# Seven block products for eight in two projections of a fused attention, gating and rotation kernel

## The chip, the core and the metric

The kernel runs on one NeuronCore of a Trainium2 chip. The metric is the device time of one execution in microseconds (us), lower is better. Engines: TensorE (PE) multiplies and transposes, VectorE (DVE) and ScalarE (ACT) work element by element, GpSimd (POOL) too, SyncE (SP) issues the DMAs. Each engine works through its own list in order; semaphores tie the lists together.

## The reference

B = 8 batches of S = 576 tokens, model width 512. Cut to what is computed:

```python
# attention, twice: packed queries p over k, v; then q over the result
x = softmax(q @ softmax(p @ k.T / 8) @ v ...)            # per head, 8 heads x 64
# gating: h = relu(x @ w_in); u, v = halves of h
v_n = (v - mean(v)) / sqrt(var(v) + 1e-6)
x = (u * (w_spatial @ v_n + b_spatial)) @ w_out          # [B, 576, 512]
# rotation and mixing
theta = x @ w_theta
y = w_tok_r @ (x * cos(theta)) + w_tok_i @ (x * sin(theta))
u = x + y
out = u + relu(u @ w_ch)
```

## The kernel before

Phase 1 (about 0 to 337 us) computes the attention and the gating for each batch and stores the gated activations G, transposed, in DRAM (`Gd`, one tensor for each pair of batches). Beside it the weights, which come as 64-bit words, are turned into f32 (`cvt_tasks`, L616 to L625) and split.

f32 accuracy comes from splitting: every value is the sum of a rounded part (hi, L182, ACT) and a rest (lo, L185, DVE or POOL), and a product is three matmuls: hi hi, hi lo, lo hi.

Phase 2 (337 us to the end) runs over 36 tiles of 128 tokens: four pairs of batches, each in nine blocks of which block 4 holds the last 64 tokens of both batches. For a tile:

- `x_half`, twice: G's hi and lo (`GH`, loaded from `Gd` by `load_g`, L859, and split) times `WX`, which holds w_out and w_out @ w_theta / 2 pi side by side, 12 matmuls of 512 columns in one PSUM bank. ACT copies x out (L886); DVE takes the angle's fraction (L892, L893) and its absolute value (L895), ACT two sines (L897, L899), DVE multiplies by x (L911), ACT and DVE or POOL split the result into `z`. All of it 256 columns wide.
- `mix` (L919): all blocks of a batch times a 128-column slice of the resident weights `WR` (real and imaginary part, hi and lo; two loads of 2304 KB, L802), 27 matmuls, 18 for the 64-row block; DVE adds the bank to x (L939, L943).
- `turn` (L951): four transposes, split into `uT`. `chan` (L956): 12 matmuls with w_ch (`WC`); DVE forms u + relu (L977), SP stores the tile (L972).

The order of the work is set by `Plan`, a list scheduler that runs while the program is built: each task has an engine, a cost, a due key, operands and buffers, and of the tasks that can start soonest the one with the lowest key is written out next. `SHIFT` (L31) adds a number to the key of a named group of tasks; it is empty here. `step` gives phase 2 its keys: X (both halves of a tile), M (mix and turn) and C (chan).

Of the kernel before, what the change touches and what calls it, by code (L numbers as in the profile page):

```python
# [30 lines left out]
SHIFT = {}  # L31
# [144 lines left out]
def moe_kernel(ctx: ExitStack, tc, qT, kT, v, pT, w_in, wsT, bs, w_out,  # L176
# [10 lines left out]
    def mm(out, lhsT, rhs, start, stop):  # L187
        PE.matmul(out, lhsT, rhs, start=start, stop=stop)  # L188
# [30 lines left out]
    WRd = [dram.tile([9 * 128, S], F32, name=f"WRd{i}") for i in range(2)]  # L219
# [4 lines left out]
    WX = [const.tile([128, 4, 4, 2, 128], F32R, name=f"WX{i}") for i in range(2)]  # L224
# [16 lines left out]
    woT = wsp.tile([128, 4, DM], F32, name="woT")  # L241
    wth = wsp.tile([128, 4, DM], F32, name="wth")
# [5 lines left out]
    junk = apm.tile([128, 512], F32, name="junk")  # L248
# [36 lines left out]
    R_woT, R_wth = fixed(4), fixed(4)  # L285
    R_WX, R_wrd, R_gd = Res(), fixed(2), fixed(NPAIR)
# [200 lines left out]
    def v_part(b, key):  # L487
# [4 lines left out]
        for j in range(5):  # L492
# [23 lines left out]
            def centre(j=j):  # L516
# [158 lines left out]
    def wo_part(k, key):  # L675
        raw, g, ps = P.res("raw"), P.res("cvg"), P.res("bank")
# [29 lines left out]
    def wr_part(k, key):  # L706
# [15 lines left out]
        def st():  # L722
            for i in range(2):
                SP.dma_start(out=WRd[i][k * 128:(k + 1) * 128, :], in_=raw.t[:, i * S:(i + 1) * S])
        P.add("SP", 1.1, st, key + 5, r=[raw], w=R_wrd, size=590e3)

    def wcomb(kt, key):
        ps, wc = P.res("bank"), P.res("cvg")

        def f():  # L730
            for m in range(4):
                mm(ps.t, woT[:, m, kt * 128:(kt + 1) * 128], wth[:, m, :], m == 0, m == 3)
        rx = Res()
        wv = lambda: wc.t[:, 0:DM].rearrange("p (d n) -> p d n", d=4)
        P.add("PE", 3.45, f, key, r=[R_woT[kt], *R_wth], new=[ps])
        P.add("ACT", 0.62, lambda: A.activation(out=wc.t[:, 0:DM], in_=ps.t, func=AF.Copy, scale=1.0 / (2 * math.pi)),
              key + 1, r=[ps], new=[wc])
        P.add("ACT", 0.62, lambda: hi(WX[0][:, kt, :, 1, :], wv()), key + 2, r=[wc], w=[rx, R_WX])
        P.add(TT, 0, lambda e: lo(WX[1][:, kt, :, 1, :], wv(), WX[0][:, kt, :, 1, :], ENG[e]), key + 3, r=[wc, rx], w=[R_WX],
              port=True)  # L740
# [32 lines left out]
    cv += [(wr_part, k) for k in range(9)]  # L773
    for n, (f, k) in enumerate(cv):
        P.group = n
        f(k, at(0, 20 + 12.5 * n))
    for kt in range(4):
        P.group = kt
        wcomb(kt, at(7, 18 + kt))

# [15 lines left out]
    def load_wr(i):  # L796
        wp = gpool(f"wr{i}")
        if not i:
            WR64.append(wp.tile([128, 9, 128], F32R, name="WR64"))
        WR.append(wp.tile([128, 9, 512], F32R, name=f"WR{i}"))  # L800
        x = WRd[i].rearrange("(k p) t -> p k t", p=128)
        SP.dma_start(out=WR[i].bitcast(F32), in_=x[:, :, 0:512])  # L802
        SP.dma_start(out=WR64[0][:, :, i * 64:i * 64 + 64].bitcast(F32), in_=x[:, :, 512:576])

    def close1():
        lbd.close()
        gp = gpool("gp")
# [3 lines left out]
    for k in range(4):
        raw = P.res("raw")

        def ld(k=k, raw=raw):
            SP.dma_start(out=raw.t, in_=Gd[0][k * 128:(k + 1) * 128, :])
        P.add("SP", 0.6, ld, at(7, 1), r=[R_gd[0]], new=[raw], size=590e3, after=[c1])
        for o in range(2):
            c, rh = slice(o * S, (o + 1) * S), Res()
            P.add("ACT", 0.69, lambda k=k, c=c, raw=raw: hi(GH[0][:, k, c], raw.t[:, c]), at(7, 20 + 2 * k + o),
                  r=[raw], w=[rh, *R_G[o:o + 2]])  # L820
            P.add("DVE", 0.76, lambda k=k, c=c, raw=raw: lo(GH[1][:, k, c], raw.t[:, c], GH[0][:, k, c]),
                  at(7, 20 + 2 * k + o), r=[raw, rh], w=R_G[o:o + 2], port=True)
# [28 lines left out]
    def load_g(p, i, key):

        c = (slice(0, 640), slice(640, 1152))[i]
        rg = R_G[0:2] if i == 0 else R_G[2:3]
        w = c.stop - c.start
        rr = fixed(4)

        def ld():
            SP.dma_start(out=GH[1][:, :, c].bitcast(F32), in_=Gd[p][:, c].rearrange("(k p) t -> p k t", p=128))  # L859
        P.add("SP", 0.6, ld, key, r=[R_gd[p]], w=[*rg, *rr], size=512 * w * 4)  # L860
        for k in range(4):
            rh = Res()
            P.add("ACT", 0.1 + w * 1.04e-3, lambda k=k: hi(GH[0][:, k, c], GH[1][:, k, c].bitcast(F32)),
                  key + 6, r=[rr[k]], w=[rh, *rg])
            P.add({"POOL": w * 2.9e-3, "DVE": 0.16 + w * 1.04e-3}, 0,
                  lambda e, k=k: lo(GH[1][:, k, c], GH[1][:, k, c].bitcast(F32), GH[0][:, k, c], ENG[e]),
                  key + 6, r=[rr[k], rh], w=rg, port=True)
# [241 lines left out]
```

## Time and profile before

| | |
|---|---|
| median of 3 runs | 882.81 us (882.39 to 882.88) |
| span of the profiled execution | 880.3 us |
| PE busy in it | 857.8 us |
| DVE, ACT, POOL busy | 555.4, 396.6, 128.8 us |
| moved by DMA | 85.98 MB, mean 98 GB/s |

The table is of one profiled execution, and 882.81 - 880.3 = 2.5 us of the median lie outside its span. Matmuls overlap, so the mean duration of one is longer than the pitch at which they follow one another; the pitch is read from the chain of waits. An engine's idle time counts only where PE waits for it.

### The profile page before, as it was taken

The numbers are of one execution on the slowest core, as the hardware profiler recorded it, in microseconds if no ns is written. First come the engines' busy times: TensorE is split into PE (matmuls) and PEld (weight loads), VectorE is DVE, ScalarE is ACT, GpSimd is POOL, SyncE is SP. The second block draws the span as 40 slices with busy tenths as digits, with TensorE's granted clock in tenths as the row PEclk, the third lists the DMA queues.
The fourth block names the chain that finished last, engine by engine and source line by source line (L and its number), as shares of the span: only waits on it lengthen the run. The fifth ranks groups of instructions, "written<-read, shape, count | busy, mean of one in ns | idle before, by whom it ended". The sixth has DMA issues, their size and how long they took to land.

```text
span 880.3 us, 14428 instructions
## 1 busy us (share of the span) xinstructions
PE 857.8 (97%) x5552; PEld 707.4 (80%) x5552; DVE 555.4 (63%) x1278; ACT 396.6 (45%) x947; POOL 128.8 (15%) x115
## 2 busy tenths in 40 slices
PE   5879999999999999999999999999999999999998
PEld 2458888889888878888888888888888888888886
DVE  5889989989847625878733752752762662652522
ACT  4777876777746633654411530520440530440300
POOL 1641103123345110122100100000100000000000
PEclk9699999999999999999999999999999999999999
DMA  9974565866400835110101200201100200000101
GB/s 332 344 258 160 179 212 202 262 207 222 150 28 28 283 104 167 60 48 1 48 1 36 84 1 25 72 1 36 66 20 16 82 0 25 36 1 0 48 1 60
DMA packets 48441, 85.98 MB, mean 98 GB/s; under 512 B 8050, under 2 KB 18546, under 8 KB 48372
## 3 DMA queue, kind: packets, MB, share of 16 engines
q1 hardware_dynamic: 48372, 85.05, 28.9%
q8 instruction: 44, 0.72, 0.3%
q14 instruction: 25, 0.20, 0.1%
HBM read 60.85 MB, written 24.18 MB: 97 GB/s over the span
## 4 chain that ended last, share of the span: by engine, by line
PE 94%; DVE 3%; ACT 1%; DMA 1%; issue 0%; SPq 0%; DVEq 0%; ACTq 0%
PE bank L188 91%; PE bank L951 2%; PE bank L372 1%; DMA woT<-w_in 1%; DVE WIN L625 0%; DMA kt<-kT 0%; ACT a L364 0%; DVE wth L621 0%; DVE one L358 0%; PE bank L691 0%; DVE t L457 0%; DVE M L185 0%; PE bank L399 0%; DVE sm L465 0%; DVE ln L509 0%
## 5 line engine op out<-in xcount | busy, mean ns | idle before, releaser
L188 PE MATMUL bank<-z,WR 128*128 128x512 f32 x1008 | 236.2, 392 | 0.0
L188 PEld LDWEIGHTS bank<-z,WR 128*128 128x128 f32 x1008 | 187.6, 188 | 38.3
L188 PE MATMUL bank<-WX,GH 128*128 128x512 f32 x864 | 200.4, 390 | 0.0
L188 PEld LDWEIGHTS bank<-WX,GH 128*128 128x128 f32 x864 | 161.5, 188 | 33.2
L182 ACT ACTIVATE uT<-bank 128x512 fp32r<-128x512 f32 x36 | 21.5, 598 | 216.9 <-PE bank L951 204.2
L188 PE MATMUL bank<-WS,VN 128*128 128x288 f32 x768 | 115.8, 298 | 0.0
L188 PEld LDWEIGHTS bank<-WS,VN 128*128 128x128 f32 x768 | 105.8, 188 | 8.2 <-issue 4.3
L188 PE MATMUL bank<-WC,uT 128*128 128x512 f32 x432 | 103.0, 391 | 0.0
L188 PEld LDWEIGHTS bank<-WC,uT 128*128 128x128 f32 x432 | 80.6, 188 | 16.6
L939 DVE TENSOR_TENSOR xs<-bank,xs 128x512 f32<-128x512 f32 x32 | 22.1, 691 | 112.1 <-PE bank L188 112.1
L185 POOL TENSOR_TENSOR z<-ab,z 128x256 fp32r<-128x256 f32 x24 | 17.7, 738 | 377.1 <-ACT z L182 377.1
L188 PE MATMUL bank<-M,at 128*128 128x512 f32 x240 | 59.6, 402 | 0.0
L897 ACT ACTIVATE ab<-ab,halfpi 128x256 f32<-128x256 f32 x72 | 36.6, 508 | 47.2 <-DVE ab L895 47.0
L188 PE MATMUL bank<-at,M 128*128 128x288 f32 x384 | 55.9, 301 | 0.0
L977 DVE SCALAR_TENSOR_TENSOR xs<-bank,xs 128x512 f32<-128x512 f32 (+1 forms) x37 | 25.0, 677 | 47.4 <-PE bank L188 47.4
L188 PEld LDWEIGHTS bank<-M,at 128*128 128x128 f32 x240 | 45.0, 192 | 12.1 <-issue 2.0
L188 PEld LDWEIGHTS bank<-at,M 128*128 128x128 f32 x384 | 51.9, 188 | 1.6 <-issue 1.0
L886 ACT ACTIVATE xs<-bank 128x256 f32<-128x256 f32 x72 | 26.9, 380 | 57.2 <-PE bank L188 43.1
L892 DVE TENSOR_SCALAR fr<-bank 128x256 f32<-128x256 f32 x72 | 30.3, 421 | 28.8 <-ACT xs L886 24.3
L605 DVE TENSOR_TENSOR gs<-bank,ur 128x288 f32<-128x288 f32 x60 | 25.8, 443 | 20.7 <-PE bank L188 20.6
L182 ACT ACTIVATE z<-ab 128x256 fp32r<-128x256 f32 x64 | 26.7, 417 | 21.4 <-DVE ab L911 21.1
L911 DVE TENSOR_TENSOR ab<-xs,ab 128x256 f32<-128x256 f32 x64 | 28.1, 439 | 9.9 <-ACT ab L897 9.8
(146 smaller groups left out, 1161.1 us busy)
## 6 DMA issues: line engine op xcount, KB each, us to landing
kt<-kT SPq DMA_DIRECT2D x16, 576.0 KB, 4.9
q<-qT SPq DMA_DIRECT2D x16, 576.0 KB, 7.1
vr<-vL SPq DMA_DIRECT2D x16, 512.0 KB, 6.3
out<-xs SPq DMA_DIRECT2D x31, 256.0 KB, 2.0
WRd<-raw SPq DMA_DIRECT2D x18, 288.0 KB, 2.6
Gd<-gs SPq DMA_DIRECT2D x16, 288.0 KB, 2.4
WR<-WRd SPq DMA_DIRECT2D x2, 2304.0 KB, 11.3
GH<-Gd SPq DMA_DIRECT2D x3, 1280.0 KB, 5.9
```

Of the source, the lines that this page charges most:

```text
L182: A.activation(out=out, in_=in_, func=AF.Copy)
L185: (eng or V).tensor_tensor(out=out, in0=in_, in1=h, op=ALU.subtract)
L188: PE.matmul(out, lhsT, rhs, start=start, stop=stop)
L372: PE.transpose(p1.t[:, k * 128:(k + 1) * 128], a1.t[:, k * 128:(k + 1) * 128], ident)
L605: P.add("DVE", 0.43, lambda c=c, ps=ps: V.tensor_tensor(out=g.t[:, c * CH:(c + 1) * CH], in0=ps.t[:, :CH], in1=ur.t[:, c, :], op=ALU.mult) ...
L886: P.add("ACT", 0.37, lambda: A.activation(out=two(xs.t[:, c]), in_=pv()[:, :, 0, :], func=AF.Copy), k2, r=[ps], w=[rx, xs, z] if one else ...
L892: V.tensor_scalar(out=two(f.t), in0=phi, scalar1=MAGIC, scalar2=MAGIC, op0=ALU.add, op1=ALU.subtract)
L897: P.add("ACT", 0.49, lambda: A.activation(out=ab.t, in_=ab.t, func=AF.Sin, bias=halfpi, scale=-2 * math.pi), k2 + 0.2, r=[ab], w=[ab])
L911: P.add("DVE", 0.43, lambda zf=zf: V.tensor_tensor(out=zf.t, in0=xs.t[:, c], in1=zf.t, op=ALU.mult), k2 + 0.3 + q, r=[rx, zf], w=[zf], por ...
L939: P.add("DVE", 0.69, lambda: V.tensor_tensor(out=xs.t, in0=ps.t, in1=xs.t, op=ALU.add), key, r=[ps, xs], w=[xs])
L951: PE.transpose(pt.t[:, d * 128:(d + 1) * 128], xs.t[:, d * 128:(d + 1) * 128], ident)
L977: lambda c=c: V.scalar_tensor_tensor(out=xs.t[:, c], in0=ps.t[:, c], scalar=0.0, in1=xs.t[:, c], op0=ALU.max, op1=ALU.add), key + CC, r=[p ...
```

## The change

Of the 36 tiles, taken in the same order, the first six keep eight block products for two tiles (`x_tile`). The other 30 form 15 pairs (`x_pair`). With two tiles as rows and the two halves of the inner dimension as columns, the product of a pair with the weights is a 2 x 2 block product, done after Strassen and Winograd with seven products: four sums of the token blocks (`load_pair`, on DVE, after four loads of 512-byte runs from `Gd`) and four sums of weight blocks (`wx_split`, through DRAM `Td`, loaded into `WX` by `wx_sums` behind the last of the six tiles). A product is six matmuls. Three PSUM banks hold a pair: in A1 four products pile up one after the other, in B1 one, in C1 two, and between products ACT copies the bank out or DVE adds it to what was copied.

Further: the rotation is 512 columns wide, and ACT takes the absolute value; POOL no longer splits `z`; w_ch is converted in phase 1; the conversions are due 11 us apart and no longer 12.5; the mixing weights lie in DRAM so that a slice of 128 output tokens is one contiguous run per partition, and `load_w` fetches each when it is due, 18 in all, into two buffers (`wrs`) in place of the two resident loads; ACT's squares for the variance go to a PSUM bank; `SHIFT` has about 170 entries. In number PE's matmuls go from 4818 to 4728, DVE's instructions from 1280 to 1172, ACT's from 885 to 842, POOL's from 120 to 97, SP's from 235 to 334.

```diff
-SHIFT = {}
+SHIFT = {
+    "chan DVE": {0: -30, 18: -8.5},
+    "chan mms": {0: 15, 13: -14.5, 17: -12, 19: 31.5, 38: 46.5},
...
+    "x_tile mms": {0: 2.5},
+}
...
-        f(k, at(0, 20 + 12.5 * n))
+        f(k, at(0, 20 + 11 * n))
...
+                P.add("SP", 0.6, lambda a=a, kk=kk, l=l: SP.dma_start(
+                    out=l().bitcast(F32), in_=Td[2 * a + kk].rearrange("p (s n) -> p s n", s=4)),
+                    key, r=[R_td[2 * a + kk]], w=[rt, R_B12], size=524e3)
+                P.add("ACT", 1.1, lambda h=h, l=l: hi(h(), l().bitcast(F32)), key + 2, r=[rt], w=[rh])
+                P.add({"POOL": 2.7, "DVE": 1.25}, 0, lambda e, h=h, l=l: lo(l(), l().bitcast(F32), h(), ENG[e]), key + 3,
+                      r=[rh], w=[rt], port=True)
...
+        def ld():
+            for s in range(2):
+                SP.dma_start(out=low(s), in_=src(pa, ja, 2 * s))
+            SP.dma_start(out=four()[:, 0], in_=src(pb, jb, 0))
+            SP.dma_start(out=low(2), in_=src(pb, jb, 2))
+        P.add("SP", 2.2, ld, key, r=[R_gd[pa], R_gd[pb]], new=[gp, g4], size=524e3, after=[])
+
+        def sums(e):
+            g, s = ENG[e], lambda n: four()[:, n]
+            g.tensor_tensor(out=s(2), in0=low(0), in1=s(0), op=ALU.subtract)
+            g.tensor_tensor(out=s(0), in0=s(0), in1=low(2), op=ALU.add)
+            g.tensor_tensor(out=s(1), in0=s(0), in1=low(0), op=ALU.subtract)
+            g.tensor_tensor(out=s(3), in0=low(1), in1=s(1), op=ALU.subtract)
...
+        def prod(s, t, bank, k, start):
+            def mms():
+                m = 0
+                for kk in range(2):
+                    for x, y in ((0, 0), (0, 1), (1, 0)):
+                        mm(bank.t, gp.t[:, x, s, kk], WX[y][:, t, kk], start and m == 0, m == 5, not start)
+                        m += 1
...
+        prod(0, 0, A1, 0, True)
+        out(0, 0, A1, 1.4, False)
+        prod(1, 1, B1, 1.4, True)
+        out(0, 0, B1, 2.8, True)
+        prod(4, 4, A1, 2.8, False)
+        out(0, 1, A1, 4.2, False)
+        prod(3, 3, C1, 4.2, True)
+        prod(5, 5, A1, 5.6, False)
+        out(1, 1, A1, 7, False)
+        out(1, 1, C1, 7.2, True)
+        prod(2, 6, A1, 7.6, False)
+        out(1, 0, A1, 9, False)
+        prod(6, 2, C1, 9, False)
+        out(0, 1, C1, 10.4, True)
...
+        P.add("ACT", 0.62, lambda: A.activation(out=ab.t, in_=f.t, func=AF.Abs), key + 0.1, r=[f], w=[ab])
...
+        P.add("SP", 0.6, lambda: SP.dma_start(out=w.t.bitcast(F32), in_=WRd[i]), key, r=[R_wrd], new=[w], size=1.18e6)
```

Where the order moves. **PE at the start of phase 2.** Before, the last half tile of the first blocks (`bank<-WX,GH`) and then the first mix, whose matmuls follow the tiles of `z`:

```order
1957 L188 MATMUL bank_160<-WX_70,GH_3487 128x512
1958 L188 MATMUL bank_160<-WX_70,GH_3486 128x512
1959 L188 MATMUL bank_160<-WX_71,GH_3486 128x512
1960 L188 MATMUL bank_160<-WX_70,GH_3487 128x512
1961 L188 MATMUL bank_165<-z_3897,WR_3495 128x512
1962 L188 MATMUL bank_165<-z_3897,WR_3744 128x512
1963 L188 MATMUL bank_165<-z_3897,WR_3495 128x512
1964 L188 MATMUL bank_165<-z_3898,WR_3495 128x512
```

After, the end of the 64-row mix (`WR_3830`), the transposes of the first mixed tile (L1190), a mix with the second slice (`wrszp_4173`), and the first pair's first two products (`gpwrp` holds the pair's blocks):

```order
1910 L259 MATMUL bank_167<-zzp_4167,WR_3830 128x512 x4
1911 L1190 MATMUL bank_169<-ident,xswtn_3873 128x128 x4
1912 L259 MATMUL bank_168<-zwtn_3885,wrszp_4173 128x512 x3
1913 L259 MATMUL bank_168<-zwtn_3886,wrszp_4173 128x512 x6
1914 L259 MATMUL bank_168<-zwtn_3887,wrszp_4173 128x512 x6
1915 L259 MATMUL bank_168<-zzp_4166,wrszp_4173 128x512 x6
1916 L259 MATMUL bank_168<-zzp_4167,wrszp_4173 128x512 x6
1917 L259 MATMUL bank_164<-WX_3533,gpwrp_3832 128x512
1918 L259 MATMUL bank_164<-WX_3534,gpwrp_3832 128x512
1919 L259 MATMUL bank_164<-WX_3533,gpwrp_3832 128x512 x2
```

The first mix now comes behind six whole tiles and runs without half tiles between, and the first transposes stand 45 matmuls behind its start.

A little further on, two pairs (`gpwrp`, `gpgp`) are interleaved; bank_164 is the A1 of the first:

```order
1937 L259 MATMUL bank_164<-WX_3533,gpwrp_3832 128x512
1938 L259 MATMUL bank_166<-WX_3533,gpgp_3535 128x512
1939 L259 MATMUL bank_166<-WX_3534,gpgp_3535 128x512
1940 L259 MATMUL bank_166<-WX_3533,gpgp_3535 128x512 x2
1941 L259 MATMUL bank_166<-WX_3534,gpgp_3535 128x512
1942 L259 MATMUL bank_166<-WX_3533,gpgp_3535 128x512
1943 L259 MATMUL bank_169<-WX_3533,gpgp_3535 128x512
1944 L259 MATMUL bank_169<-WX_3534,gpgp_3535 128x512
1945 L259 MATMUL bank_169<-WX_3533,gpgp_3535 128x512 x2
1946 L259 MATMUL bank_169<-WX_3534,gpgp_3535 128x512
1947 L259 MATMUL bank_169<-WX_3533,gpgp_3535 128x512
1948 L259 MATMUL bank_164<-WX_3533,gpwrp_3832 128x512
```

Between two uses of bank_164 stand two products of the other pair.

**SP at the same place.** Before, the block loads of the first pair of batches (L815), the resident weights (L802, L803) and stores of G (L593):

```order
162 L815 DMA raw_149<-Gd_59 128x1152
163 L802 DMA WR_3495<-WRd_63 128x9x512
164 L803 DMA WR_3494<-WRd_63 128x9x64
165 L815 DMA raw_150<-Gd_59 128x1152
166 L593 DMA Gd_62<-gs_146 128x576
167 L593 DMA Gd_62<-gs_147 128x576
168 L802 DMA WR_3744<-WRd_64 128x9x512
169 L803 DMA WR_3494<-WRd_64 128x9x64
```

After, the last store of G, two weight slices, a pair's four blocks, and the four weight sums:

```order
203 L668 DMA Gd_62<-cvg_155 128x64
204 L1160 DMA wrszp_4172<-WRd 128x2304
205 L1160 DMA wrszp_4173<-WRd 128x2304
206 L1022 DMA gpgp_3535<-Gd_59 128x2x128 x2
207 L1023 DMA g4wrp_3833<-Gd_60 128x2x128
208 L1024 DMA gpgp_3535<-Gd_60 128x2x128
209 L847 DMA WX_3534<-Td 128x4x256 x4
210 L1160 DMA wrszp_4172<-WRd 128x2304
```

The weights are fetched behind the last store of G, and the blocks and weight sums behind them.

**DVE at the same place.** Before, the first mix's add (L939) stands among rotations and the conversion of w_ch:

```order
733 L892 TENSOR_SCALAR fr_3919<-bank_160 128x256
734 L893 TENSOR_TENSOR fr_3919<-bank_160,fr_3919 128x256
735 L939 TENSOR_TENSOR xs_3914<-bank_165,xs_3914 128x512
736 L895 SCALAR_TENSOR_TENSOR ab_3922<-fr_3919 128x256
737 L185 TENSOR_TENSOR WC_3896<-xs_3911,WC_3895 128x256
```

After, it stands (L1178) behind a pair's sums (L1030 to L1032) and lo parts, and the next one behind three lo parts of the weight sums (`WX`), which wait for the loads from `Td`:

```order
686 L1032 TENSOR_TENSOR g4wrp_3833<-gpgp_3535,g4wrp_3833 128x256
687 L256 TENSOR_TENSOR gpgp_3535<-gpgp_3535 128x768
688 L1178 TENSOR_TENSOR xswtn_3873<-bank_166,xswtn_3873 128x512
689 L256 TENSOR_TENSOR WX_3534<-WX_3534,WX_3533 128x4x256 x3
690 L256 TENSOR_TENSOR uTzp_4170<-bank_169,uTzp_4170 128x512
691 L256 TENSOR_TENSOR gpgp_3535<-g4wrp_3833,gpgp_3535 128x1024
692 L1182 TENSOR_TENSOR xswtn_3872<-bank_167,xswtn_3872 64x512 x2
693 L1178 TENSOR_TENSOR xswtn_3876<-bank_168,xswtn_3876 128x512
```

The add that the second transposes need now stands behind work that hangs on DMAs.

## Rows read from the trace of the kernel before

**Rows 1.** Busy time, share of the span and instructions of an engine, page.

```profile
PE 857.8 (97%) x5552; PEld 707.4 (80%) x5552; DVE 555.4 (63%) x1278; ACT 396.6 (45%) x947; POOL 128.8 (15%) x115
```

**Rows 2.** PE in order of time: start us, us, work [idle before and its releaser].

```profile
5.12 3.59 PE L188 MATMUL bank<-kt,pk 64*32 64x288 f32 x32 [5.12 <-DMA kt<-kT]
...
21.89 0.68 PE L188 MATMUL bank<-kt,pk 64*32 64x288 f32 x4 [2.27 <-DMA kt<-kT]
...
33.41 8.68 PE L188 MATMUL bank<-M,at 128*128 128x512 f32 x30
...
56.70 0.90 PE L188 MATMUL bank<-vr,aT 128*32 128x64 f32 x40 [0.52 <-ACT aT L378]
...
290.91 7.41 PE L188 MATMUL bank<-M,at 128*128 128x512 f32 x30
```

**Rows 3.** Windows: bounds, length, busy us (instructions) by engine, clock, DMA share, GB/s.

```profile
22.00:44.00 22.00, 18.08 (x131) 10.66 (x128) 18.92 (x39) 16.87 (x41) 15.33 (x11) 0.69 1.02 344
...
132.00:176.00 44.00, 44.00 (x471) 38.00 (x468) 41.75 (x97) 31.23 (x77) 10.44 (x8) 1.00 0.71 232
...
503.00:586.00 83.00, 83.00 (x377) 68.79 (x376) 48.35 (x110) 30.29 (x74) 2.95 (x4) 1.00 0.10 34
```

**Rows 4.** The chain of waits: start us, us, piece and its number of instructions.

```profile
244.71 157.84 PE bank L188 x926
...
451.15 4.12 PE bank L188 x18
455.27 0.44 PE bank L951 x4
455.70 6.16 PE bank L188 x27
...
477.52 44.92 PE bank L188 x198
...
865.66 10.93 PE bank L188 x48
```

**Rows 5.** Costliest groups: line, engine, operation, out<-in, number | busy, mean ns | idle before.

```profile
L188 PE MATMUL bank<-WX,GH 128*128 128x512 f32 x864 | 200.4, 390 | 0.0
```

**Rows 6.** DVE's groups from 337 us on, same columns.

```profile
L895 DVE SCALAR_TENSOR_TENSOR ab<-fr 128x256 f32<-128x256 f32 x72 | 32.9, 460 | 1.0
L893 DVE TENSOR_TENSOR fr<-bank,fr 128x256 f32<-128x256 f32 x72 | 30.6, 425 | 2.5
...
L939 DVE TENSOR_TENSOR xs<-bank,xs 128x512 f32<-128x512 f32 x32 | 22.1, 691 | 112.1 <-PE bank L188 112.1
...
L185 DVE TENSOR_TENSOR GH<-GH,GH 128x640 fp32r<-128x640 f32 x8 | 6.2, 816 | 0.0
```

**Rows 7.** ACT's groups from 337 us on, same columns.

```profile
L897 ACT ACTIVATE ab<-ab,halfpi 128x256 f32<-128x256 f32 x72 | 36.6, 508 | 47.2 <-DVE ab L895 47.0
L899 ACT ACTIVATE fr<-fr 128x256 f32<-128x256 f32 x72 | 29.0, 403 | 0.0
L886 ACT ACTIVATE xs<-bank 128x256 f32<-128x256 f32 x72 | 26.9, 380 | 57.2 <-PE bank L188 43.1 <-DVE fr L893 7.4 <-DMA out<-xs 3.6
...
L182 ACT ACTIVATE uT<-bank 128x512 fp32r<-128x512 f32 x36 | 21.5, 598 | 216.9 <-PE bank L951 204.2 <-PE bank L188 12.7
L182 ACT ACTIVATE GH<-GH 128x640 fp32r<-128x640 f32 x12 | 8.1, 729 | 4.1 <-DMA GH<-Gd 4.1
```

**Rows 8.** DMA issues: out<-in, engine, number, KB each, median us to landing.

```profile
WR<-WRd SPq DMA_DIRECT2D x2, 2304.0 KB, 11.3
```

**Rows 9.** Windows at the end of phase 1, columns of rows 3.

```profile
322.00:326.00 4.00, 4.00 (x32) 4.00 (x32) 0.46 (x1) 0.45 (x2) 0.34 (x1) 1.00 0.59 162
326.00:330.00 4.00, 4.00 (x32) 4.00 (x32) 1.00 (x3) 0.00 (x0) 0.00 (x0) 1.00 1.04 399
330.00:334.00 4.00, 4.00 (x32) 4.00 (x31) 1.19 (x3) 0.00 (x0) 0.00 (x0) 1.00 0.91 255
```

**Rows 10.** One of POOL's groups from 337 us on, columns of rows 5.

```profile
L185 POOL TENSOR_TENSOR GH<-GH,GH 128x640 fp32r<-128x640 f32 x4 | 6.7, 1707 | 15.2 <-ACT GH L182 15.2
```

More of the change, by code (lines that the diff above doesn't have):

```diff
@@ L722, in st @@
         def st():
[L723 to L740, printed above, removed]
+            for x in range(2):
+                SP.dma_start(out=WRd[:, :, k, x, :].rearrange("i p t -> p i t"),
+                             in_=raw.t[:, x * S:x * S + 512].rearrange("p (i t) -> p i t", i=4))
+                SP.dma_start(out=W64d[:, k, x, :], in_=raw.t[:, x * S + 512:(x + 1) * S])
@@ L810, in moe_kernel @@
     c1 = P.add("SP", 0.0, close1, at(7, 0), after=done1)
[L811 to L822, printed above, removed]
@@ L831, in moe_kernel @@
-    wspools = {"vf", "ur", "gs", "raw", "cvg", "ln"}
-    fixed3 = {*R_VN.values(), *R_ws, *R_woT, *R_wth, *R_spare, R_WX}
+        p = gpool("wrp")
+        WR64.append(p.tile([128, 9, 2, 64], F32R, name="WR64"))
+        SP.dma_start(out=WR64[0].bitcast(F32), in_=W64d)
+        grow(p, gp=1, g4=1)
+    R_W64 = Res()
+    c2 = P.add("SP", 0.6, close2, at(7, 10), r=[R_wrd], w=[R_W64], size=0.59e6, after=[*done2, c1])
+    BLOCKS = (4, 0, 1, 2, 3, 5, 6, 7, 8)
+    TILES = [(p, j) for p in range(NPAIR) for j in BLOCKS]
@@ new lines, in moe_kernel, with load_tile @@
+    wx_all, R_B12 = [*R_WX.values()], Res()
+    def load_tile(t, key, gp=None):
+        s, new, h = 0 if gp is None else 2, gp is None, Res()
+        gp, l = gp or P.res("gp"), Res()
+        p, j = TILES[t]
+        x = lambda i: gp.t[:, i, s:s + 2]
+        def ld():
+            for n in range(2):
+                SP.dma_start(out=x(1)[:, n].bitcast(F32), in_=Gd[p][n * 256:(n + 1) * 256, j * 128:(j + 1) * 128].rearrange(
+                    "(k p) t -> p k t", p=128))
+        P.add("SP", 1.2, ld, key, r=[R_gd[p]], w=[l] if new else [gp, l], new=[gp] if new else [], size=262e3)
+        P.add("ACT", 0.62, lambda: hi(x(0), x(1).bitcast(F32)), key + 4, r=[gp, l], w=[h])
+        P.add("DVE", 0.71, lambda: lo(x(1), x(1).bitcast(F32), x(0)), key + 5, r=[h], w=[l], port=True)
+        return gp, s, [gp, h, l]
@@ new lines, in moe_kernel, with closet @@
+    loaded, N1 = {}, 3
+    for t in range(4):
+        P.group = t
+        loaded[t] = load_tile(t, at(7, 6 + 3 * t), loaded[t - 1][0] if t % 2 else None)
+    wtpools = {"vf", "raw"}
+    fixedt = {*R_woT, *R_wth, *R_woR, *R_spare}
+    donet = [t for t in P.tasks if any(x.pool in wtpools or x in fixedt for x in t.res)]
+    def closet():
+        pwt.close()
+        grow(gpool("wtn"), xs=8, fa=5, z=3)
+    ct = P.add("SP", 0.0, closet, at(7, 11), after=[*donet, c2])
+    wspools = {"ur", "gs", "cvg", "ln"}
@@ L845, in moe_kernel @@
-    c3 = P.add("SP", 0.0, close3, at(7, 11), after=[*done3, P.tasks[-1]])
+        grow(gpool("zp"), xs=2, z=4, uT=2, wrs=2)
+    c3 = P.add("SP", 0.0, close3, at(7, 11), after=[*done3, ct])
     T2 = at(8, 20)
-    R_WC = Res()
     TQ = {"POOL": 0.8, "DVE": 0.43}
[L851 to L867, printed above, removed]
@@ new lines, in step @@
+        key = clock
+        if kind == "x":
+            t = TILES[a]
+            P.group = 10 * t[0] + t[1]
+            xs[t], z[t] = P.res("xs"), P.res("z")
+            x_tile(a, key, xs[t], z[t])
+            if a % 2 and a + 4 < 2 * N1:
+                for n in range(a + 3, a + 5):
+                    loaded[n] = load_tile(n, key + 5.4, loaded[n - 1][0] if n % 2 else None)
+            elif a % 2 and a // 2 + 2 < NX:
+                P.group = a // 2 + 2
+                loaded[a // 2 + 2] = load_pair(a // 2 + 2, key + 5.4)
+            clock += 5.4
+            return
@@ new lines, in step @@
+        if kind == "M":
+            if i < 4 and i not in held:
+                held[i] = load_w(i, key - 8)
+            mix(o, i, [z[p, 4], *(z[p, 5 * o + n] for n in range(4))], key, xs[p, j], held.get(i))
+            clock += MX if i < 4 else HX
+            if i < 4 or o:
+                uT[p, j] = P.res("uT")
+                turn(key + (MX if i < 4 else HX), xs[p, j], uT[p, j])
+        else:
+            chan(p, o, i, key, xs[p, j], uT[p, j], 2 if a + 1 == B and i == LAST else 1)
+            clock += CC
@@ new lines, in moe_kernel, with more @@
+    LAST = 0
+    held = {}
+    nx = 0
+    def more(n):
+        nonlocal nx
+        while nx < min(n, NX):
+            if nx < N1:
+                step("x", 2 * nx)
+                step("x", 2 * nx + 1)
+            else:
+                step("X", nx)
+            nx += 1
+            if nx == N1:
+                wx_sums(clock - 4)
+    need = [3, 5, 7, 9, 12, 14, 16, 18]
+    more(3)
+    tail = None
+    for b in range(B):
+        odd = b % 2
+        I = (3, 2, 1, 0) if odd else (0, 1, 2, 3)
+        ahead = need[min(b + 1, B - 1)]
+        step("M", b, I[0])
+        if tail is not None:
+            step("C", b - 1, tail)
+        more(min(ahead, nx + 1))
+        step("M", b, I[1])
+        for i in I[:2]:
+            held.pop(i)
+        step("M", b, 4)
+        step("C", b, I[0])
+        more(min(ahead, nx + 1))
+        step("M", b, I[2])
+        step("C", b, I[1])
+        if odd:
+            step("C", b, 4)
+        more(ahead)
+        step("M", b, I[3])
+        step("C", b, I[2])
+        tail = I[3]
```

447 lines of the change are left out of this document (283 added, 164 removed).

## The prediction

> **What bounds the kernel now.** First the busy table: TensorE (PE) works 857.8 of 880.3 us, VectorE (DVE) 555.4 [rows 1]. PE's list in order of time tells where the rest lies: its waits add up to 18.75 us, the first is 5.12 us for the first keys, and the last, 0.52 us, ends at 56.7 us [rows 2]. 857.8 + 18.75 + 3.7 us behind PE's last matmul (it ends at 865.66 + 10.93 = 876.6) = 880.3. So from 57 us on PE never waits. The windows agree: 44.00 of 44 us and 83.00 of 83 at a granted clock of 1.00, 2.4 GHz; only 22 to 44 us shows 0.69 [rows 3], where 30 matmuls took 8.68 us that take 7.41 later [rows 2]. The chain of waits then gives a matmul's pitch: 926 in 157.84 us and 198 in 44.92 are both 0.227 us [rows 4]. A 512-wide matmul taken out after 57 us is worth 0.227 us if nothing new makes PE wait. The profiled span is 880.3 us against a median of 882.8, so 2.5 us lie around it; I add them at the end.
>
> **The change part by part.** *Seven products for eight.* A tile had two groups of 12 matmuls, 48 for two tiles. A pair now has seven products of 6, that is 42; 15 pairs save 6 x 15 = 90. No other matmul is added or taken: mixing keeps 1008, the channel product 432, the transposes 144. 90 x 0.2269 = **20.4 us** off. The groups' row, 200.4 us / 864 = 0.232 [rows 5], would give 20.9, but ends of matmuls are modelled there, so I take the pitch. A rule of the Trainium skill weighs against that: "TensorE: Matmul & The Clock Gate", section "Wait — 56ns, not 53.3ns?", gives 215.7 ns between starts of 512-wide matmuls at 2.4 GHz. By it the term would be 19.4 us and the time 1.0 us higher; the trace has 226.9 ns, and the measurement decides.
>
> *What the saved products cost other engines.* The four sums of token blocks (128x256, 0.44 us each, by DVE's 128x256 adds at 425 and 460 ns), their hi and lo parts (768 and 1024 columns: 0.95 and 1.2 us on DVE by 816 ns for 640; nearly the same on ScalarE (ACT), 729 ns) and six adds of 425 ns come per pair; the rotation gets cheaper, since a 512-wide operation costs 691 where two of 256 cost 850 to 920, and the absolute value (460 ns twice a tile) leaves DVE for ACT. For a tile, DVE before: 2 x 7 operations of about 0.44 = 6.1 and 0.7 for its share of the block loads, 6.8 us; after: six operations of up to 0.69 = 4.1, three adds 1.3, two sums 0.9, half of 0.95 + 1.2 = 1.1, 7.3 us. ACT before: 2 x (380 + 508 + 403 ns and two of 0.41) + 0.6 = 4.8; after: four copies 1.5, five of 0.6 to 0.7 = 3.2, half of 0.85 + 1.1 = 1.0, 5.7 us [rows 6, 7]. So DVE gets 15 and ACT 27 us more over 30 tiles. In 503 to 586 us DVE is busy 48.35 and ACT 30.29 of 83 [rows 3]: hidden, cost 0. If that cover were gone, DVE's 15 us would be the price.
>
> *Reading a bank between products.* Three times a pair bank A1 is read by ACT and then accumulated into again, and C1 once by DVE. PE must wait there until the two copies (380 ns each [rows 7], 0.76 us) are over. The order always puts at least one product, 6 x 0.227 = 1.36 us, mostly two or more, between two uses of one bank. ACT is an in-order queue: its 72 copies of before waited 7.4 us for DVE and 3.6 us for a DMA [rows 7], 0.15 us each. 0.76 + 0.15 is under 1.36: cost 0, upper bound 60 hand-offs x 0.15 = 9 us if nothing lay between.
>
> *The transition to phase 2.* This is the one place where I expect a new wait. Count from PE's last gating matmul, when the buffers that hold the weight slices come free. SP then issues two slices (1152 KB each), a pair's four blocks (512 KB) and four loads of weight sums (2048 KB), 4864 KB or 4.98 MB. PE meanwhile has 48 products, a slice of 27, the 64-row block's 18, four transposes and a slice of 27: 10.9 + 6.16 + 4.12 + 0.44 + 6.16 = 27.8 us [rows 4]. The first transposes wait for a DVE add that stands behind the block sums; the next ones, 12 matmuls (2.7 us) later, for an add behind three weight lo parts, a uT lo, a 1024-wide lo and two 64-row adds. From the last byte to that add it is 1.1 (ACT) + 1.2 + 4.0 = 6.3 us, so the bytes must have landed at 27.8 + 2.7 - 6.3 = 24.2 us: 206 GB/s. The rows of before: 2304 KB in 11.3 us, which is 209 GB/s; 162, 399 and 255 GB/s in three 4-us windows [rows 8, 9], 272 on average. At 272 GB/s there is spare time, at 162 it takes 30.7 us, 6.5 late. Since 209 leaves almost nothing over and SP needs time for each issue, I take **1 us**, range 0 to 6.5. "DMA: Bandwidth & Descriptors", section Specifications, in the Trainium skill has about 358 GB/s from HBM for a core, with runs of 512 B or more; the block loads have runs of exactly 512 B. By that rate the 4.98 MB take 13.9 us, the term is 0 and the time 1.0 us lower. The trace has both less (162) and more (399) and no loads of 512-B runs.
>
> *Slices later on.* 18 loads of 1152 KB, two buffers. A slice is due every 30 us or so and takes 5.7 us by the row above; the DMA share in phase 2 is 0.10 [rows 3]. Cost 0. Each SP instruction that waits for a buffer holds up the stores behind it; those have to be home only when their buffer is used again, two tiles later.
>
> *Phase 1.* New: 16 subtractions of 128x256, the conversion of w_ch (before in phase 2) and more stores; some lo parts go to POOL. By rows of the same shapes DVE gets about 8.7 us more, most of it after 241 us. In 132 to 176 us it is busy 41.75 of 44 [rows 3], the tightest place. With conversions spread differently I put the cost at 0; the bound is 8.7 us, if all of it fell where DVE is nearly full and PE waited for all. The sums are on DVE and not on POOL, where 640 columns take 1707 ns [rows 10].
>
> *The start.* New keys move first operations (the first q logits ahead of a weight product, one load of w_in ahead of v). The releasers are those of before: keys, the softmax on ACT, WIN and M on DVE. 13.6 us of waits besides the first could shrink or grow. I take 0; gain up to 6 us (nearly half of them), loss up to 4 (two waits like the 2.27 us one [rows 2]).
>
> Sum: 880.3 - 20.4 + 1 = 860.9, + 2.5 = **863.4 us**.
>
> **The rivals.** (a) *The transition starves*: at 162 GB/s PE comes 6.5 us late instead of 1: 869. For it: six transfers at once, of which four only then become free to start. Against: 399 GB/s nearby. To eat the whole gain it would have to last 24.2 + 20.4 = 44.6 us, 112 GB/s, less than any loaded window shows. (b) *Phase 1 turns DVE-bound*: place 88 to 220 us, 5 to 9 us late: 868 to 872. For it: 95% busy. Against: 2.25 us idle in each such 44 us without a single wait of PE. (c) *The start gains more*: 857 to 859. (d) *Slower than before: the hand-offs of bank A1*. If ACT's queue, which stands behind sines that wait for DVE, gives the copies late, PE waits in each of 15 pairs. From 20.4 / 15 = 1.36 us a pair on, or 0.34 us at each of the four hand-offs, the gain is gone. At a cover of 1.36 us and 0.76 us of copies each must start 0.6 + 0.34 = 0.94 us late on average, six times the 0.15 us of the row. At 2 us a pair it is 863.4 + 30 = 893, and pauses like those of 22 to 44 us, where the clock was 0.69, would add to it. (e) That the matmuls are not saved is out: the order has 90 fewer.
>
> **How the numbers follow.** Forecast (860 to 867.5): 0.60. (a) 0.12, (b) 0.08, (c) 0.10, (d) 0.07, mixtures of (a), (b) and (d) from 873 to 881 0.03. This kernel can tell about 0.2% (1.8 us) from no change. Faster: 0.60 + 0.12 + 0.08 + 0.10 and most of the mixtures = 0.91; same 0.02; slower 0.07. The range takes in the start's gain of 6 us (857.5) and, above, (a), (b) and the start's loss on top of 1 us: 863.4 + 5.5 + 4 = 873. What is left out is (d), the mixtures and a little at the lower end, under 2 in 10.
>
> **What would show it.** After: 4728 matmuls; PE busy about 837 us; a pitch of 0.227 us; chain pieces in phase 2 without pieces of ACT or DVE in a pair; waits of PE at the first two groups of transposes of at most 1 to 2 us; the start's waits 13 to 23 us in all. Wrong it is if PE's waits list ACT copies into xs or fa (d), WX or wrs loads with over 3 us (a), or DVE lines between 88 and 220 us (b).

## The result and the profile after

The changed kernel took 867.88 us (median of 4, 866.88 to 869.04) against 882.85; the ratio is 0.9832 with a 95% interval of 0.9818 to 0.9846, so 14.8 us or 1.7% less, far outside the interval. That is inside the range, and 4.5 us over the forecast of 863.4; it lies just above the band of 860 to 867.5 to which the prediction gave 0.60.

The profiled execution spans 866.9 us, 13.4 less than the one before. That is less than the 15.0 between the medians because the profiled execution of the kernel before was a short one (880.3 us, where 24 of its 25 executions beside the experiments span 880.7 to 882.2) and this one is among the longer (865.0 to 867.2). The page's first part, columns as in [rows 1]:

```profile
PE 841.6 (97%) x5462; PEld 693.1 (80%) x5462; DVE 574.6 (66%) x1170; ACT 421.0 (49%) x904; POOL 117.2 (14%) x92
```

PE is busy 16.2 us less, not 20.4. DVE has 19 and ACT 24 us more; the prediction had 15 and 27 for phase 2 alone. PE's list of waits (engine, line, waited for: us in all, times, longest):

```profile
PE bank L259 <- DMA kt<-kT: 7.0, 3, 5.5
PE bank L449 <- ACT a L441: 6.1, 2, 5.3
PE bank L259 <- ACT aT L455: 2.3, 4, 0.9
PE bank L476 <- ACT pd L473: 2.1, 3, 1.1
PE bank L259 <- DVE WIN L702: 1.8, 2, 1.3
PE bank L1190 <- DVE xswtn L1178: 1.4, 1, 1.4
PE bank L259 <- DVE M L256: 0.6, 1, 0.6
```

Before, no wait on the softmax exponentials (`a`) was over 1.3 us. In order of time, as in [rows 2]:

```profile
5.48 3.43 PE L259 MATMUL bank<-kt,pk 64*32 64x288 f32 x32 [5.48 <-DMA kt<-kT]
...
34.17 1.17 PE L449 MATMUL bank<-ident,a 128*128 128x128 f32 x4 [5.28 <-ACT a L441]
...
39.06 2.91 PE L259 MATMUL bank<-M,at 128*128 128x512 f32 x6
...
101.22 0.33 PE L476 MATMUL bank<-ident,pd 128*128 128x128 f32 x1 [0.44 <-ACT pd L473]
...
140.18 0.33 PE L476 MATMUL bank<-ident,pd 128*128 128x128 f32 x1 [1.13 <-ACT pd L473]
...
386.92 0.66 PE L1190 MATMUL bank<-ident,xswtn 128*128 128x128 f32 x4 [1.44 <-DVE xswtn L1178]
```

The matmuls with M, which ran from 33.41 us before [rows 2], now begin at 39.06. Three places have new waits: the start, phase 1 (with a third, small one at 255 us they make 1.8 us there), and the transition. The waits up to 66 us add up to 18.2 us, hardly another sum than the 18.75 of before. Windows of the start and of the two places at which the prediction looked, columns as in [rows 3]:

```profile
0.00:22.00 22.00, 12.94 (x174) 6.56 (x176) 11.18 (x28) 9.26 (x25) 2.84 (x9) 0.77 0.94 331
22.00:44.00 22.00, 14.76 (x149) 8.20 (x146) 19.24 (x37) 13.61 (x32) 14.68 (x10) 0.53 1.06 355
...
132.00:176.00 44.00, 42.87 (x412) 35.66 (x411) 38.32 (x93) 30.10 (x67) 16.39 (x13) 1.00 0.73 236
...
503.00:586.00 83.00, 83.00 (x379) 68.89 (x378) 40.84 (x73) 26.47 (x53) 0.00 (x0) 1.00 0.29 94
```

The granted clock is lower at the start (0.92 and 0.69 before in these two windows), and PE is full in phase 2 from the first pairs on. There the chain of waits has the pitch of before, 26.55 / 117 = 0.2269 us, and no ACT or DVE piece between pairs:

```profile
496.77 26.55 PE bank L259 x117
```

### The profile page after: what moved, and what is told of

It reads as the page before. It is cut to its first block, busy times and chain, and to the rows that moved or that the text cites. A ratio compares the mean times of both kernels' runs of the same rounds, so it can differ in the third digit from the quotient of the medians.

```text
span 866.9 us, 14188 instructions
## 1 busy us (share of the span) xinstructions
PE 841.6 (97%) x5462; PEld 693.1 (80%) x5462; DVE 574.6 (66%) x1170; ACT 421.0 (49%) x904; POOL 117.2 (14%) x92
## 4 chain that ended last, share of the span: by engine, by line
PE 90%; DVE 4%; ACT 3%; DMA 1%; issue 1%; POOL 0%; DVEq 0%; SPq 0%; ACTq 0%; POOLq 0%
PE bank L259 86%; PE bank L1190 2%; PE bank L449 1%; DMA raw<-w_out 1%; DMA kt<-kT 0%; ACT vf L621 0%; ACT VN L253 0%; PE bank L476 0%; DVE g4wrp L1032 0%; DVE t L534 0%; DVE wth L698 0%; ACT WIN L693 0%; ACT M L253 0%; DVE zzp L256 0%; DVE ln L608 0%
## 5 line engine op out<-in xcount | busy, mean ns | idle before, releaser
L259 PE MATMUL bank<-zzp,wrszp 128*128 128x512 f32 x504 | 124.2, 390 | 0.0
L259 PEld LDWEIGHTS bank<-zzp,wrszp 128*128 128x128 f32 x504 | 94.5, 188 | 19.6
L259 PE MATMUL bank<-WC,uTzp 128*128 128x512 f32 x432 | 103.6, 391 | 0.0
L259 PE MATMUL bank<-WX,gpgp 128*128 128x512 f32 x390 | 95.5, 391 | 0.0
L259 PE MATMUL bank<-WX,gpwrp 128*128 128x512 f32 x384 | 94.6, 393 | 0.0
L259 PEld LDWEIGHTS bank<-WC,uTzp 128*128 128x128 f32 x432 | 80.7, 188 | 16.6
L259 PE MATMUL bank<-zwtn,wrszp 128*128 128x512 f32 x360 | 91.4, 391 | 0.0
L259 PEld LDWEIGHTS bank<-WX,gpgp 128*128 128x128 f32 x390 | 72.5, 188 | 14.5
L259 PEld LDWEIGHTS bank<-WX,gpwrp 128*128 128x128 f32 x384 | 71.2, 188 | 14.3
L259 PEld LDWEIGHTS bank<-zwtn,wrszp 128*128 128x128 f32 x360 | 67.1, 188 | 13.5
L1178 DVE TENSOR_TENSOR xswtn<-bank,xswtn 128x512 f32<-128x512 f32 x26 | 17.9, 689 | 68.8 <-PE bank L259 68.7
```

Source lines behind the costliest of these rows:

```text
L259: PE.matmul(out, lhsT, rhs, start=start, stop=stop, skip_group_check=more)
L1178: P.add("DVE", 0.69, lambda: V.tensor_tensor(out=xs.t, in0=ps.t, in1=xs.t, op=ALU.add), key, r=[ps, xs], w=[xs])
```

## The experiments

**What 90 matmuls are worth by themselves.** The kernel before, with every order kept:

```diff
-        ps, f, ab = (P.res(n) for n in ("bank", "fr", "ab"))
+        ps, f, ab, n = *(P.res(n) for n in ("bank", "fr", "ab")), 9 if e and P.group not in (4, 0, 1, 2, 3, 5) else 12
...
-                    mm(ps.t, GH[x][:, k, j * 128:(j + 1) * 128],
+                    m < n and mm(ps.t, GH[x][:, k, j * 128:(j + 1) * 128],
```

> The kernel before with 90 matmuls fewer and nothing else: in the second half of 30 of the 36 tiles the last 3 of 12 matmuls of x and theta are left out (so x and theta of those tiles lack a part of their sum); order, DMAs and the other engines are as before. Theory of the prediction (a matmul is worth its pitch of 0.227 us because PE never waits after 57 us): 20.4 us less, 862.4. If PE had waits that the profile hides, or another engine stood just behind it, the saving would be smaller: 15 us or less, 868 and up, near the 867.9 of the change. By the mean of the groups, 0.232 us, it would be 20.9; by 215.7 ns 19.4.

862.68 us against 883.53 beside it, ratio 0.9765 (0.9752 to 0.9779): 20.8 us less, 19.5 to 21.9 by the interval. PE waited nowhere after 57 us. The term of 20.4 holds. The Trainium skill, "TensorE: Matmul & The Clock Gate", section "Wait — 56ns, not 53.3ns?", gives 215.7 ns between starts, and by it the term would be 19.4 us. That lies just under the interval, as the measured pitch of 226.9 ns already said.

**The wait at the transition.** One of the four lo parts of the weight sums goes from POOL to DVE:

```diff
-                P.add({"POOL": 2.7, "DVE": 1.25}, 0, lambda e, h=h, l=l: lo(l(), l().bitcast(F32), h(), ENG[e]), key + 3,
+                P.add({"DVE": 1.25}, 0, lambda e, h=h, l=l: lo(l(), l().bitcast(F32), h(), ENG[e]), key + 3,
```

> The changed kernel with the one lo part of the weight sums that POOL does (128x1024, 2.42 us at 382 to 386 us) on DVE like the other three. Theory P (POOL's operation held up DVE's block sum, which took 2.50 us in place of 0.42, and so the first transposes): that sum takes 0.42 us again, PE's wait of 1.44 us there is gone, and the time falls by 1.0 to 1.5 us. Theory D (the DMAs of the transition are late, as the prediction had it): DVE waits for loads at the same place, the wait of PE stays at 1 us or more, and the time does not change or rises by up to 1.2 us, the lo part that DVE now does before the second transposes.

First the changed kernel: DVE in order of time around the wait, then POOL's one row there.

```profile
382.21 0.42 DVE L1031 TENSOR_TENSOR g4wrp<-g4wrp,gpgp 128x256 f32<-128x256 f32 x1
382.67 2.50 DVE L1032 TENSOR_TENSOR g4wrp<-gpgp,g4wrp 128x256 f32<-128x256 f32 x1
385.31 0.96 DVE L256 TENSOR_TENSOR gpgp<-gpgp 128x768 fp32r<-128x768 f32 x1
386.18 0.68 DVE L1178 TENSOR_TENSOR xswtn<-bank,xswtn 128x512 f32<-128x512 f32 x1
```

```profile
382.47 2.42 POOL L256 TENSOR_TENSOR WX<-WX,WX 128x1024 fp32r<-128x1024 f32 x1 [45.01 <-ACT WX L253]
```

The last block sum took 2.50 us, while its like took 0.42 just before: it ended at 385.17, 0.28 us after POOL's operation of 2.42 us. And with the lo part on DVE:

```profile
382.40 0.43 DVE L1031 TENSOR_TENSOR g4wrp<-g4wrp,gpgp 128x256 f32<-128x256 f32 x1
382.86 0.43 DVE L1032 TENSOR_TENSOR g4wrp<-gpgp,g4wrp 128x256 f32<-128x256 f32 x1
383.42 0.96 DVE L256 TENSOR_TENSOR gpgp<-gpgp 128x768 fp32r<-128x768 f32 x1
384.30 0.69 DVE L1178 TENSOR_TENSOR xswtn<-bank,xswtn 128x512 f32<-128x512 f32 x1
```

PE's wait there is gone, and none takes its place behind the added operation. The time was 867.21 us, ratio 0.9809 (0.9796 to 0.9823). Against the changed kernel that is 0.7 us by the medians and 2.0 by the ratios, on different chips; theory P's 1.0 to 1.5 lies between, and the trace decides for it. The DMAs were not what ended last. From 366.4 us, when the two slices were issued, the changed kernel's window shows 323 GB/s:

```profile
366.00:386.00 20.00, 19.48 (x86) 15.80 (x85) 15.63 (x23) 12.32 (x24) 2.42 (x1) 1.00 0.94 323
```

A store and the next weight slice are in that figure. The last of the four weight sums was issued at 376.8 us, and none of them took more than 7.2 us to land, so the bytes were there by 384.0; by the prediction's count they were needed 24.2 us after the last gating matmul, which ended at 364.4, so at 388.6. The Trainium skill has the hold-up in "SBUF — State Buffer", section "SBUF: two separate sides": DVE operations with two SBUF inputs and POOL operations that read SBUF hold one pair of ports in turn, each for a whole instruction. This trace agrees, 2.42 us of POOL for 2.08 us more on DVE.

**The keys of phase 1.** `SHIFT` keeps its phase-2 names alone:

```diff
-    "cvt_tasks a": {0: -7.5, 3: -30.5},
...
-    "ws_part ACT": {2: -19.5},
-    "ws_part bias": {2: -2.19},
-    "ws_part ld": {0: -2.5, 2: -3},
```

> The changed kernel without the entries of SHIFT that name groups of phase 1 (attention, gating, conversions); those of phase 2 stay. Theory S (the new keys cost time at the start: the 5.28 us wait at 34.17 us and the clock that stays at half from 12 to 42 us): the first 66 us come out as before, 18.8 us of PE waits and a clock of about 0.92 and 0.69 in the first two 22-us windows, and the time falls by 3 to 5 us, to 863 to 865. Rival K (the keys were what held phase 1 together with the added conversions, and without them DVE or POOL makes PE wait): more waits of PE between 66 and 340 us, and the time rises, by 2 to 10 us.

864.47 us, ratio 0.9786 (0.9772 to 0.9799): 3.4 less by the medians, 4.1 by the ratios. That is theory S. No wait is left between 57 us and the transition, so the added conversions and the subtractions do not make PE wait without these keys. ACT in order of time, the changed kernel and then this one:

```profile
29.51 0.68 ACT L253 ACTIVATE WS<-raw 128x576 fp32r<-128x576 f32 x1
30.08 0.26 ACT L554 ACTIVATE t<-t 128x64 f32<-128x64 f32 x1
30.23 0.68 ACT L253 ACTIVATE WSA<-raw 128x576 fp32r<-128x576 f32 x1
30.80 0.73 ACT L253 ACTIVATE at<-f 128x640 fp32r<-128x640 f32 x1
31.56 0.68 ACT L253 ACTIVATE WSB<-raw 1x576 fp32r<-1x576 f32 x1
32.26 0.68 ACT L253 ACTIVATE cvg<-raw 1x576 fp32r<-1x576 f32 x1
32.96 0.67 ACT L693 ACTIVATE WIN<-woT 128x512 f32<-128x512 f32 x1
33.54 0.48 ACT L441 ACTIVATE a<-bank,one 128x288 f32<-128x288 f32 x1
```

```profile
29.12 0.51 ACT L393 ACTIVATE a<-bank,one 128x288 f32<-128x288 f32 x1
```

The third exponentials start 4.4 us earlier without the keys. ACT's list is not the whole of it. They need DVE's maxima of the logits, which also moved; DVE's rows, the changed kernel and then this one (27.73 us in the kernel before):

```profile
30.36 0.80 DVE L435 TENSOR_REDUCE one<-bank 128x1 f32<-128x288 f32 x2
```

```profile
27.77 0.75 DVE L387 TENSOR_REDUCE one<-bank 128x1 f32<-128x288 f32 x2
```

So 2.6 of the 4.4 us came over DVE's list, and the other 1.8 over ACT's, where three conversions still stood in front when the maxima were done (31.4 us).

**The same keys in the kernel before.** Only `SHIFT` is filled, with those of attention, gating and conversions (`sub`, `th_part`, `wc_part`, `wo_part` and `wr_part` are not among them):

```diff
-SHIFT = {}
+SHIFT = {"cvt_tasks a": {0: -7.5, 3: -30.5}, "cvt_tasks b1": {0: -28, 1: 20.5, 2: 21.5, 4: -11.5, 6: -18, 10: -39, 19: 7, 20: -22},
...
```

> The kernel before with the phase-1 keys of the change and nothing else of it (eight products, resident weights, conversions 12.5 us apart). Theory S (the keys themselves cost, through the order of the first 60 us): 2 to 4 us more than before, 885 to 887, with a wait near 5 us at the third transposes and a clock at or near half from 12 to 42 us. Rival (the cost comes from keys and the other edits of phase 1 together): within 1 us of 883.5.

887.20 us against 882.54, ratio 1.0048 (1.0033 to 1.0063): 2.9 to 5.6 us more, a little over theory S. The wait of 5.28 us stands at the same place, and two new ones came:

```profile
34.86 1.17 PE L372 MATMUL bank<-ident,a 128*128 128x128 f32 x4 [5.28 <-ACT a L364]
...
79.36 1.84 PE L188 MATMUL bank<-WS,VN 128*128 128x288 f32 x12 [1.33 <-DVE M L185]
...
391.88 3.06 PE L188 MATMUL bank<-WX,GH 128*128 128x512 f32 x12 [1.21 <-ACT xs L886]
```

So these keys cost by themselves, without the new work. Not all of it falls in the first 60 us, as theory S had it: the two new waits, 2.5 us together, lie behind them, and up to 66 us PE's idle time is 19.8 us against 18.8 before.

**Which of the keys.** Two attempts to narrow it. Without the keys of the conversion of w_spatial alone:

```diff
-    "ws_part ACT": {2: -19.5},
-    "ws_part bias": {2: -2.19},
-    "ws_part ld": {0: -2.5, 2: -3},
+    "ws_part ACT": {},
+    "ws_part bias": {},
+    "ws_part ld": {},
```

> The changed kernel without the keys of ws_part alone (three names, four entries), by which the conversion of w_spatial stands in ACT's list ahead of the third exponentials. Theory W (these put 5 ACT operations before the exponentials, and PE's wait of 5.28 us follows): the exponentials come 1.3 us or more earlier, that wait falls under 4 us, and 1 to 3 of the 3.4 us that the phase-1 keys cost come back, 865 to 867. Rival: the wait is set by DVE's maxima in front of the exponentials and the matmuls with M that came later, and the time stays within 0.5 us of 867.9.

867.34 us, and the wait went from 5.28 to 4.33 us. Theory W's signs did not come (a wait under 4 us, exponentials 1.3 us earlier), and the time is 0.5 us lower by the medians, at the edge of what the rival allowed. But the edit did not clear ACT's list; other operations of the same conversion took the places:

```profile
30.10 0.69 ACT L253 ACTIVATE WS<-raw 128x576 fp32r<-128x576 f32 x1
30.68 0.26 ACT L554 ACTIVATE t<-t 128x64 f32<-128x64 f32 x1
30.82 0.68 ACT L253 ACTIVATE WS<-raw 128x576 fp32r<-128x576 f32 x1
31.39 0.73 ACT L253 ACTIVATE at<-f 128x640 fp32r<-128x640 f32 x1
32.02 1.25 ACT L253 ACTIVATE WS<-raw 128x576 fp32r<-128x576 f32 x2
33.17 0.49 ACT L441 ACTIVATE a<-bank,one 128x288 f32<-128x288 f32 x1
```

The exponentials came only 0.4 us earlier, so this run does not tell how much of the wait is owed to ACT's list. Without the keys of the start and with the later ones:

```diff
-    "m_part ACT": {0: -35},
-    "m_part DVE": {0: -2.5, 1: -5.76, 3: 3, 5: -20.5, 6: -12},
...
+    "m_part ACT": {},
+    "m_part DVE": {3: 3, 5: -20.5, 6: -12},
...
```

> The changed kernel without the phase-1 keys of the start (all of win_part and ws_part, the lowest batches of the attention and gating parts, the conversions up to the fourth); the later phase-1 keys stay. If the start alone costs: the time is that without any phase-1 keys, 864.5, and the two waits of 0.44 and 1.13 us at 101 and 140 us go or stay by themselves. If the later keys carry a part (those two waits, 1.57 us): 865.5 to 866.

869.72 us, outside both expectations. The wait of 5.28 us is gone, yet five others between 139 and 256 us came, 0.48, 0.23, 1.20, 0.55 and 1.03. That fits a scheduler that takes each step from what is ready then: half of a set of keys led to a third order and not to half of the effect. Which keys cost what stays open.

**Copies twice.** ACT copies each bank of a pair out two times:

```diff
-                for a in range(2):
+                for a in (0, 1, 0, 1):
                     A.activation(out=to[a].t[:, c], in_=bank.t[:, a * 256:(a + 1) * 256], func=AF.Copy)
```

> The changed kernel with ACT's copies out of a pair's banks done twice (120 more of 128x256, 0.38 us each, 45.6 us on ACT), so that each of the 60 hand-offs takes 1.52 us and no longer 0.76. Theory of the prediction (at least one product of 1.36 us, mostly two or more, lies between two uses of a bank): hidden but for the few places with a single product, 0 to 3 us more. Rival (d) (hand-offs are at the edge already): 0.76 us for each of 60, up to 46 us more, with ACT copies in PE's list of waits.

868.16 us, ratio 0.9825 (0.9812 to 0.9839). ACT was busy 453.9 us in place of 421.0, so each of the 60 hand-offs became 0.55 us longer, not 0.76, since copies that follow one another overlap (0.38 us each, starts 0.28 us apart or less). PE's list of waits has the same seven lines as the changed kernel's, and no copy among them. The hand-offs have a spare of at least 0.55 us everywhere; rival (d), which needed 0.34 us of waiting at each, is out.

**Waits or clock.** The changed kernel once more, with both mended beside it on the same chip, and each with a filler in PE's wait at the third exponentials:

```diff
-            for k in range(4):
-                PE.transpose(p1.t[:, k * 128:(k + 1) * 128], a1.t[:, k * 128:(k + 1) * 128], ident)
+            for k in range(-10 if (b, q) == (1, 0) else 0, 4):
+                mm(p1.t, VB[:, 0:128], VB, True, True) if k < 0 else PE.transpose(p1.t[:, k * 128:(k + 1) * 128], a1.t[:, k * 128:(k + 1) * 128], ident)
```

> The changed kernel again, on the chip of the three runs beside it, so that they can be compared without a difference between chips. Within 1 us of 867.9, with the clock of the first 44 us varying between executions (0.77 and 0.53, or 1.00 and 0.61 in the two 22-us windows, have been seen for this start).

868.04 us. Its profiled execution had another clock at the start than the first one, and the same span, 866.8 us:

```profile
0.00:22.00 22.00, 13.74 (x172) 7.04 (x173) 10.58 (x27) 8.66 (x24) 2.47 (x9) 1.00 0.95 327
22.00:44.00 22.00, 12.45 (x151) 7.81 (x152) 19.88 (x39) 14.45 (x33) 15.07 (x11) 0.69 1.06 357
```

With 1.00 and 0.69 for 0.77 and 0.53, PE was done with its work sooner and waited longer: 19.7 us up to 66 us, not 18.2. That fits a start that is as long as its chain over DMA, DVE and ACT makes it.

> The changed kernel with ten matmuls of 128x512 without use (their result is overwritten by the transposes behind them) in PE's list where it waits 5.28 us for the third exponentials; nothing else moves. At half clock ten take 4.3 us, so they fit the wait. Theory C (most of what the phase-1 keys cost is the clock: PE's dense work with M starts at 39.4 us in place of 33.4, and up to it and 3 us beyond all matmuls run at half clock): the clock rises before 39 us, the 44 matmuls behind that wait take half, and the time falls by 1.5 to 3 us against the changed kernel on the same chip. Rival O (the waits themselves and the order cost the time, the clock nothing): unchanged, or up to 0.5 us more where the filler runs past the exponentials.

867.25 us, ratio 0.9815 (0.9802 to 0.9829). The clock did rise in the wait, to 1.00 in 32 to 36 us where it had been 0.50, and was 0.77 in the whole window:

```profile
22.00:44.00 22.00, 16.14 (x163) 10.08 (x160) 19.70 (x36) 14.19 (x34) 15.20 (x11) 0.77 1.06 359
```

It gave 0.8 us by the medians, not resolved by the intervals, and not the 1.5 to 3 of theory C. The clock is at most a small part of the cost.

**Both mended.** Without the phase-1 keys and with all four lo parts on DVE, on two chips:

> The changed kernel without the phase-1 keys and with all four lo parts of the weight sums on DVE. The two findings so far are in different places, the first 60 us and 378 to 386 us. If they add up: PE waits nowhere after 57 us, 864.5 - 1.0 to 1.5 = 863.0 to 863.5 us. If the wait at the first transposes only gives way to one behind the DVE operation that is added before the second transposes: 864 to 865.

> The changed kernel without the phase-1 keys and with all lo parts of the weight sums on DVE, again, on the same chip as the change. If the two findings stand, 4.0 to 5.0 us under the changed kernel beside it.

863.48 us (ratio 0.9783, 0.9768 to 0.9798) and 863.81 us (0.9779, 0.9765 to 0.9792), on the second chip 4.2 us under the changed kernel beside it. It beats both kernels: 0.5% under the change. PE's whole list of waits of the second:

```profile
PE bank L211 <- DMA kt<-kT: 7.7, 3, 5.3
PE bank L211 <- DVE WIN L654: 2.7, 3, 1.2
PE bank L211 <- ACT aT L407: 2.5, 4, 0.9
PE bank L401 <- ACT a L393: 2.4, 3, 1.3
PE bank L428 <- ACT pd L425: 2.0, 2, 1.5
PE bank L211 <- DVE M L208: 0.5, 1, 0.5
```

All of it lies before 59 us.

> The version with both findings mended, with four matmuls of 128x512 without use in PE's wait of 1.27 us at 29 us, ahead of the third transposes. Theory C: the clock, at half from 24 to 36 us there, rises some us earlier, 0 to 1.5 us less. Rival O: four matmuls at half clock are 1.7 us and run past the end of a wait of 1.27, so 0 to 0.5 us more.

863.67 us: four filler matmuls there neither help nor harm, by as much as these runs can tell.

## Why the prediction was right, and where it was 4.5 us off

The two profiled executions of the last comparison, on one chip, split most of the difference. The change spans 866.8 us, the mended version 862.0, 4.8 us less. PE's waits are 19.7 against 17.8 us up to 66 us, 2.1 against 0 in phase 1 behind that, and 1.4 against 0 at the transition, together 5.5 more; PE's busy time is 0.8 less. So the phase-1 keys cost about 1 us net at the start and 2 us later in phase 1, and the transition costs 1.4. The mended version lies 0.1 and 0.4 us above the forecast without the 1 us of the transition; these runs do not resolve what is left.

- *Seven products for eight*, 20.4 us: right. 20.8 measured alone, and the mended version has 19.1 and 19.3 against before, with intervals between 17.8 and 20.8 us that hold 20.4.
- *Cover on DVE and ACT* and *reading a bank between products*, both 0: right. PE has no wait in phase 2 after 387 us, and copies done twice cost nothing that shows.
- *The transition*, 1 us: 1.44 us, at the transposes that the prediction named, but for another reason, so that the term came near is luck. The sum of bytes was right, and they landed 4.6 us before they were needed. What it left out was that the fourth lo part is POOL's, and that this POOL operation held up a DVE operation: 2.08 us. PE's stretch from the last gating matmul is otherwise as counted, 21.1 us for 21.2.
- *Phase 1*, 0 us: this step failed, with 1.8 to 2.1 us of waits. Not DVE's fill, as rival (b) had it: in 132 to 176 us DVE is busy less than before, and the waits end with ACT. They are gone without the phase-1 keys; the prediction had priced the added work there, and not the new order.
- *The start*, 0 us with a loss of up to 4: this step failed for the same reason. The keys moved the third exponentials 4.4 us back, and the matmuls with M 5.7 us back on PE, although the sum of the waits hardly changed. The prediction named two moves among the first operations and bounded the gain by nearly half of the waits and the loss by two waits of 2.27 us. It did not follow the lists of DVE and ACT, in which the maxima come 2.6 us later and the third exponentials go from place 25 to 31. The phase-1 keys cost 3.4, 3.7 and 4.7 us in all by the medians of three pairs (the change without them, the change with the lo part on DVE without them, the kernel before with them), and 4.1, 2.3 and 4.2 by the ratios.

One sign failed too: PE busy was to be about 837 us and is 841.6. It is 840.6 even in the kernel before with 90 matmuls fewer, since PE's busy time in the first 66 us changes with the execution (46.2 and 47.7 us for two executions of the changed kernel).

No rival came about as it was described. That the range held is owed to its upper end, into which the loss at the start had been taken.

## What to carry to other kernels

Matmuls taken out of a stretch without waits are worth their pitch, and an experiment that leaves the same number out of the old kernel shows it in one run. A list of new priorities has to be followed on every engine up to the last place where PE still waits, since a change of order that looks small on one engine can put several operations before the one that another waits for; and removing half of such a list need not give half of its effect. Where DVE works on a deadline with operands in SBUF, an operation on POOL that reads SBUF can cost it most of that operation's length, here 2.08 of 2.42 us.

## What had not been expected of the hardware

A DVE sum of 128x256 took 2.50 us beside a POOL operation of 2.42 us, and 0.43 without it. At the start, the granted clock differed between executions of one kernel, 0.77 and 0.53 or 1.00 and 0.69 in the first two 22-us windows, with spans of 866.9 and 866.8 us: where a chain over other engines sets the length, PE's clock and PE's waits trade against each other.
